# A chunked scan and a feed-forward layer on one core: the lead-in issued from one written list

## The chip, the core and the metric

The kernel runs on one core of a Trainium2 chip. The core has a matrix engine, TensorE (PE in the rows, with its weight loads as PEld), a vector engine, VectorE (DVE), a scalar engine, ScalarE (ACT), GpSimd (POOL), and SyncE (SP), which only issues transfers here. Each engine works through its own list of instructions in order; semaphores make one wait for another. The metric is the device time in microseconds (us), median of several runs of the same program.

## The reference

Two layers stand one behind the other. The first is a scan over 768 positions with a decay for each, for 4 batches and 8 heads of 32 columns (D), with a state of 16 x 32 for each head (N = 16). The reference does it in chunks:

```
log_a = log(clip(a, 1e-6, 1));  cum = cumsum(log_a) inside a chunk
L = exp(cum_i - cum_j) for i >= j, else 0
y = ((C B^T) * L) x  +  exp(cum_i) * (C state)
state = exp(cum_end) * state + sum_j exp(cum_end - cum_j) B_j x_j
```

The second takes the 3072 tokens of 256 columns that the first gives, and computes `g = max(0.01 h, h)` with `h = x @ w_in` (256 to 2048 columns), and then `g @ w_out` (2048 to 256).

## The kernel before

**The scan** goes in 16 chunks of 48 positions, 0 to 15, one behind the other, since each needs the state of the one before. A chunk takes these steps, with the lines of before:

- decays: ones are added up by matmuls to sums of logarithms (`sc` or `pd` in PSUM), and ScalarE takes the exponential to `lt`. Chunks 0 to 2 are "direct": VectorE fills tiles `reach` (L595) that a matmul turns into sums (L272 to L299). Chunks 3 and on take their sums from rows in DRAM: the sums are computed once (`sums`), split into three bf16 parts (`split_sums`), stored (`left_d`, `right_d`, L240 and L244), and loaded for each chunk as small rows `dl` and `dr` (L253 and L256) into one of SLOTS = 2 places. A "decay block" is the pair of matmuls of L280 that works on them. ScalarE fills the rest of such a place with constants (L209, "a fill").
- scores: C B^T of all heads, 32 matmuls (L336, "score block"); C comes in with the chunk's input `bcn`. Each head's C has to stand in its own half of the partitions with zeros in the other. Chunks 0 to 2 get a narrow C, which ScalarE copies twice with a factor of 0 or 1 for each partition (`spread_c`, L315, into `cs`); the other chunks get it spread from the host, as a wider input `d_l`.
- weigh: VectorE multiplies scores by decays, into `lt` (L350); GpSimd does the same for the part of the state (L321).
- chunk products: 64 matmuls `lt` by `xs` (L366).
- handing on: VectorE transposes the new state into `stage` (L396), and eight small copies put it into the next chunk's `xs` (L412); before, ScalarE, VectorE and GpSimd share them by a written tuple.
- the result goes to `xh` (L423, rounded to the high part) and `xl` (L431, the rest), the tokens of the second layer.

**The feed-forward layer** works on tiles of 512 tokens (t, 6 of them) and blocks of 128 of the 2048 inner columns (f, 16 of them), in *steps* 0, 1, 2 and on of one (t, f) each. The first steps are tile 0 with the weight blocks 0 to 5; they need chunks 0 to 2 only. For each step there are: the first-layer product, six matmuls of 512 columns into `hp` (L522); the leaky activation into `gh` (L529) and `hp` (L532) on ScalarE; the low part `gl` on VectorE (L535); and the second-layer product, six matmuls into `op` (L546), some steps later. The weights come as 64-bit words, and are decoded once per block: magnitude (L450 on ScalarE or L463 on VectorE), shift, sign and low word on VectorE (L468 to L477), then the high part `wh` on ScalarE (L490) and the low part `wl` on GpSimd (L491).

**Order.** The program is written out in the order in which each engine runs it; nothing is moved by a scheduler. Before, a straight piece of code (L575 to L713, "the lead-in") issues the work up to the third chunk, and then a loop over the steps issues each step with what goes beside it: the chunks' products, the decays two chunks ahead, the decoding. In its first five steps (EARLY) the loop takes other branches than later. Two more matmuls on a tile of zeros stand ahead of step 1's product (BRIDGE, issued by `keep_warm`, L119, "the bridging matmuls").

**Transfers** all go through SyncE's one queue: inputs `bcn` (three buffers), `xs` (two buffers), weights `raw` (three buffers), the rows. A transfer into a buffer that is still in use makes SyncE wait, with all that is behind it.

## Time and profile before

| | |
|---|---|
| median of 3 runs | 304.93 us (304.08 to 305.57) |
| the profiled execution | 303.38 us, of which the span from the first to the last instruction is 301.5 us |
| TensorE busy | 293.6 us, 97% of the span, 2718 instructions |
| VectorE busy | 218.3 us, 72%, 379 instructions |
| ScalarE busy | 182.4 us, 61%, 351 instructions |
| GpSimd busy | 71.9 us, 24%, 148 instructions |
| transfers | 22.95 MB, mean 76 GB/s |

The shares are means over the whole span. In the page's 40 slices (7.5 us each) TensorE has 8 or 9 tenths in all but the last, GpSimd stops after the 15th, and the transfers move 160 to 315 GB/s in the first eleven slices and little later: the chunks and the decoding of weights lie in the first part, and only the feed-forward layer in the rest. So the stage around the change, the first seventh, has to be read for itself.

### The profile page before, as it was taken

How to read it: one execution, taken by the hardware profiler on the slowest of the kernel's cores; microseconds unless marked ns; L12 is line 12 of the kernel's file. 1: busy time of each engine (PE TensorE's matmuls, PEld its weight loads, DVE VectorE, ACT ScalarE, POOL GpSimd, SP SyncE). 2: the span in 40 equal slices, each digit the busy share in tenths (PEclk: the TensorE clock that was granted, in tenths of full speed). 3: DMA queues.
4: the chain of work that ended last, by engine and by line, in shares of the span. 5: the costliest groups of instructions: out<-in, count | busy, mean ns of one | idle time of the engine just before them, and what ended most of it. 6: DMA issues, size and time to landing. Idle time of an engine off the chain costs nothing.

```text
span 301.5 us, 6819 instructions
## 1 busy us (share of the span) xinstructions
PE 293.6 (97%) x2718; PEld 230.9 (77%) x2718; DVE 218.3 (72%) x379; ACT 182.4 (61%) x351; POOL 71.9 (24%) x148
## 2 busy tenths in 40 slices
PE   8889999999999999999999999999999999999995
PEld 4547676777777778888888888888888888888883
DVE  6879979987875688866877887677576565656562
ACT  6989758666755565735555666574665364536452
POOL 7567666866865440000000000000000000000000
PEclk9999999999999999999999999999999999999999
DMA  6697658665532101000100000000030000000004
GB/s 235 213 315 245 199 173 252 206 222 174 161 93 93 28 5 67 0 2 0 70 2 1 0 0 3 0 0 0 2 139 0 0 2 1 0 0 2 0 0 139
DMA packets 12492, 22.95 MB, mean 76 GB/s; under 512 B 4590, under 2 KB 5486, under 8 KB 12462
## 3 DMA queue, kind: packets, MB, share of 16 engines
q1 hardware_dynamic: 12462, 22.53, 23.2%
q8 instruction: 21, 0.34, 0.5%
q14 instruction: 9, 0.07, 0.1%
HBM read 19.08 MB, written 3.44 MB: 75 GB/s over the span
## 4 chain that ended last, share of the span: by engine, by line
PE 89%; DVE 5%; ACT 2%; issue 1%; DMA 1%; POOL 0%; SPq 0%; DVEq 0%
PE sc L776 18%; PE op L806 14%; PE sc L806 14%; PE op L546 14%; PE hp L522 13%; PE hp L776 7%; PE sc L366 3%; PE sc L336 2%; PE sc L280 1%; DVE mag L463 1%; DVE top L468 1%; DMA dr<-right_d 1%; DVE w L477 1%; DVE gl L535 1%; DVE lt L350 1%
## 5 line engine op out<-in xcount | busy, mean ns | idle before, releaser
L412 POOL COPY xs<-stage 16x128 f32<-16x128 f32 x98 | 35.8, 365 | 24.5 <-DVE stage L396 18.2
L529 ACT ACTIVATE gh<-hp 128x512 fp32r<-128x512 f32 x32 | 19.1, 598 | 26.0 <-PE hp L522 25.8
L817 ACT ACTIVATE gh<-u 128x512 fp32r<-128x512 f32 x32 | 20.0, 625 | 17.7 <-DVE u L858 17.7
L546 PE MATMUL op<-gh,wh 128*128 128x512 f32 x64 | 27.9, 436 | 0.0
L821 DVE TENSOR_TENSOR gl<-u,gh 128x512 fp32r<-128x512 f32 x32 | 22.0, 687 | 7.9 <-ACT u L818 7.9
L857 DVE TENSOR_TENSOR u<-sc,kept 128x512 f32<-128x512 f32 x16 | 11.1, 691 | 22.2 <-PE sc L776 22.2
L817 ACT ACTIVATE gh<-kept 128x512 fp32r<-128x512 f32 x16 | 10.1, 633 | 28.1 <-DVE kept L866 28.1
L817 ACT ACTIVATE gh<-hp 128x512 fp32r<-128x512 f32 x16 | 9.6, 598 | 26.8 <-PE hp L776 26.8
L546 PE MATMUL op<-gl,wh 128*128 128x512 f32 x64 | 25.2, 394 | 0.4 <-DVE gl L535 0.4
L866 DVE TENSOR_TENSOR kept<-sc,kept 128x512 f32<-128x512 f32 x16 | 11.1, 692 | 19.4 <-PE sc L776 19.3
L546 PE MATMUL op<-gh,wl 128*128 128x512 f32 x64 | 25.0, 390 | 0.0
L806 PE MATMUL op<-gl,wh 128*128 128x512 f32 x64 | 24.9, 389 | 0.0
L806 PE MATMUL sc<-gl,wh 128*128 128x512 f32 x64 | 24.9, 389 | 0.0
L806 PE MATMUL sc<-gh,wl 128*128 128x512 f32 x64 | 24.9, 389 | 0.0
L806 PE MATMUL op<-gh,wh 128*128 128x512 f32 x64 | 24.9, 389 | 0.0
L806 PE MATMUL op<-gh,wl 128*128 128x512 f32 x64 | 24.9, 389 | 0.0
L806 PE MATMUL sc<-gh,wh 128*128 128x512 f32 x64 | 24.9, 389 | 0.0
L350 DVE TENSOR_TENSOR lt<-sc,lt 128x384 f32<-128x384 f32 x32 | 16.3, 550 | 10.7 <-ACT gh L529 8.1
L535 DVE TENSOR_TENSOR gl<-hp,gh 128x512 fp32r<-128x512 f32 x32 | 21.7, 677 | 3.1 <-ACT hp L532 3.1
L491 POOL TENSOR_TENSOR wl<-w,wh 128x512 fp32r<-128x512 f32 x16 | 20.7, 1301 | 9.6 <-ACT wh L490 9.4
L522 PE MATMUL hp<-xh,wh 128*128 128x512 f32 x64 | 20.3, 398 | 0.8 <-ACT xh L423 0.6
L818 ACT ACTIVATE u<-u 128x512 f32<-128x512 f32 x32 | 20.2, 632 | 1.0
(147 smaller groups left out, 733.1 us busy)
## 6 DMA issues: line engine op xcount, KB each, us to landing
raw<-w_l SPq DMA_DIRECT2D x16, 512.0 KB, 4.1
bcn<-d_l SPq DMA_DIRECT2D x13, 448.0 KB, 5.1
xs<-x_l SPq DMA_DIRECT2D x28, 96.0 KB, 3.4
out_l<-ob SPq DMA_DIRECT2D x10, 256.0 KB, 2.0
bcn<-c_l SPq DMA_DIRECT2D x3, 352.0 KB
xs<-x_l SPq DMA_DIRECT2D x2, 256.0 KB, 5.1
out_l<-ob SPq DMA_DIRECT2D x4, 128.0 KB
dl<-left_d SPq DMA_DIRECT2D x13, 9.0 KB, 3.7
```

Of the source, the lines that this page charges most:

```text
L350: nc.vector.tensor_tensor(out=to, in0=at, in1=to, op=ALU.mult)
L412: copy(xss[c + 1][h * R:h * R + N, 2 * p:2 * p + 2, bs], stage[rows, :, bs],)
L491: nc.gpsimd.tensor_tensor(out=wl[:, f], in0=w32s[f], in1=wh[:, f], op=ALU.subtract)
L522: nc.tensor.matmul(hp, lhsT=w_half[h][:, f, k * 128:(k + 1) * 128], rhs=x[t][:, k, :], start=(n == 0), stop=(n == 5),)
L529: nc.scalar.activation(ghs[s], hp, AF.Prelu, alpha=0.01)
L535: nc.vector.tensor_tensor(out=gls[s], in0=hps.pop(s), in1=ghs[s], op=ALU.subtract)
L546: nc.tensor.matmul(op, lhsT=w_half[h][:, f, DM + m * 128:DM + (m + 1) * 128], rhs=x, start=(start and i == 0), stop=(last and i == 2),)
L776: nc.tensor.matmul(bank, lhsT=w[h], rhs=x[g], start=start and i == 0, stop=i == 2, skip_group_check=True,)
L806: nc.tensor.matmul(outs[t][m], lhsT=w_half[h][:, f, DM + m * 128:DM + (m + 1) * 128], rhs=x, start=start and i == 0, stop=last and i == 2,)
L817: nc.scalar.activation(gh, h, AF.Prelu, alpha=0.01)
L818: nc.scalar.activation(in_place, h, AF.Prelu, alpha=0.01)
L821: nc.vector.tensor_tensor(out=gl, in0=g, in1=gh, op=ALU.subtract)
```

## The change

The lead-in and the first six steps are issued from one list of names, LEAD_IN; the loop begins at step 6. A name is a piece of work and a number (`p1` is the product of chunk 1, `hp0` the first-layer product of step 0, `w2` the transfer of weight block 2), and a letter behind a colon chooses the engine (A ScalarE, V VectorE, P GpSimd). With it:

- the masks of the decays of chunks 0 to 2 come first, also the sums of the far chunks (`rev`);
- the decays of chunks 4 and 5 stand in one double block behind the first-layer product of step 0 (`hp0 ... dec4 ... dec5`), where before those of chunk 4 stood behind the product of step 1, and those of chunk 5 behind that of step 2;
- C comes spread for all chunks; `spread_c` with its copies, and the tile `mine` and its making, are gone; the inputs of chunks 0 to 2 are as wide as the others;
- `xs` has three buffers, and the x of chunk 1 comes without the rows that a state will overwrite;
- the two bridging matmuls are gone;
- engines change for some work: the fill `reach4` to GpSimd, a clearing `top0`, the rest fills of chunks 3 and 4 (`fr4:A`, `fr3:P`), the hand-on copies of chunks 0 to 5, and `wl` of the blocks 1 and 5 to VectorE.

```diff
-OUT_AT = {1: 0, 2: 1, 3: 2, 4: 3, 5: 4, 8: 5}
+OUT_AT = {8: 5}
-BRIDGE = {1: 2}
+BEGIN, DONE = 6, 7
...
+AT_ONCE = ["la", "c0", "c1", "x0", "w0"]
+LEAD_IN = """
+clampf after clampn mask0 lnf mask1 lnn sums less reach1:V reach0:V fl0 rev sel cols
+reach3:V revn erevn cast0 direct0 exp0 rest reach2:V erevf sd0 top1:P sc0 cast1 x1
+weigh0 c2 reach4:P direct1 mask2 part2 exp1 top0:P save0 p0 abs0 reach5:V turn0 h6:A sc1
+h7:A shift0 w1 weigh1 h1:P x2 fl1 h4:P h2:V h0:A highs0 sign0 h5:A direct2 lows0 sd1
+low0 w2 exp2 h3:P fr4:A p1 abs1 rows3 sc2 sd2 turn1 h11:A fr3:P shift1 h9:P weigh2 h10:A
+h15:A c3 w3 h13:A sign1 low1 h12:P h14:A h8:P highs1 p2 dec3 rows4 turn2 sc3 wh0 abs2
+lows1 highs2 wh1 lows2 h22:V wl0:P rows5 x3 shift2 c4 hp0 h17:P exp3 h18:A h16:A weigh3
+c5 dec4 w4 sign2 dec5 h19:P h21:P wl1:V sd3 abs3 h20:P h23:A shift3 gh0 low2 sign3 rows6
+exp4 act0 exp5 hp1 p3 wh2 low3 wl2:P gh1 w5 wh3 save1 gl0 x4 sc4 turn3 op0 act1 highs3
...
+"""
...
-    pxs = scan.enter_context(tc.tile_pool(name="pxs", bufs=2))
+    pxs = scan.enter_context(tc.tile_pool(name="pxs", bufs=3))
-    pcs = early.enter_context(tc.tile_pool(name="pcs", bufs=2))
...
     def fetch_c(c, eng=nc.sync):
-        ins[c] = pin.tile([128, FAR], F32, name="bcn")
-        if c < SPREAD:
-            eng.dma_start(ins[c][:, :NEAR], c_l[c])
-        else:
-            eng.dma_start(ins[c], d_l[c - SPREAD])
+        ins[c] = pin.tile([128, ALL], F32, name="bcn")
+        eng.dma_start(ins[c], c_l[c])
...
-        for rows in [slice(h * R + N, h * R + R) for h in range(2)] if c > 1 else [slice(0, 2 * R)]:
+        for rows in [slice(h * R + N, h * R + R) for h in range(2)] if c else [slice(0, 2 * R)]:
...
-    def spread_c(c):
-        if c >= SPREAD:
-            spread[c] = ins[c][:, C_AT:].rearrange("p (b e i) -> p b e i", b=NB, e=2)
-            return
-        cs = spread[c] = pcs.tile([128, NB, 2, Q], F32, name="cs")
-        src = ins[c][:, C_AT:NEAR].rearrange("p (b i) -> p b i", b=NB)
-        for e in range(2):
-            nc.scalar.activation(cs[:, :, e], src, AF.Copy, scale=mine[:, e:e + 1])
...
     def scores(c, space):
-        cs = spread[c]
+        cs = ins[c][:, C_AT:].rearrange("p (b e i) -> p b e i", b=NB, e=2)
...
+    for name in LEAD_IN.split():
+        if name in acts:
+            acts[name]()
+            continue
+        name, _, eng = name.partition(":")
+        kind = name.rstrip("0123456789")
+        i = int(name[len(kind):])
+        if eng:
+            chosen[kind](i, engines[eng])
+        else:
+            numbered[kind](i)
...
-    for s in range(total):
+    for s in range(BEGIN, total):
         c = out_at.get(s)
-        n = PASSES[s] if s < len(PASSES) else 4
-        ffn_in(s, BRIDGE.get(s, 0))
+        n = PASSES if s < NF + 3 else 4
+        ffn_in(s)
+        ffn_high(s)
```

What the list changes in the order of the instructions shows best in three places. In the rows a number behind a name tells buffers apart.

TensorE, from the product of chunk 2 (`pd<-lt,xs`) to the first-layer product of step 1, before; the three `hp` rows of a product read xh by wh, xl by wh, xh by wl:

```order
L366 MATMUL pd_421<-lt_337,xs_280 32x64 x32
L522 MATMUL hp_489<-xh_328,wh_163 128x512 x2
L522 MATMUL hp_489<-xl_329,wh_163 128x512 x2
L522 MATMUL hp_489<-xh_328,wl_164 128x512 x2
L280 MATMUL sc_501<-dr_133,dl_132 128x384
L336 MATMUL sc_504<-bcn_289 64x96 x16
L119 LDWEIGHTS idle_101
L119 MATMUL hp_548<-idle_101 128x512
L522 MATMUL hp_548<-xh_328,wh_163 128x512 x2
```

The same place after (line numbers of the changed kernel):

```order
L377 MATMUL pd_404<-lt_322,xs_300 32x64 x32
L301 MATMUL sc_437<-dr_124,dl_123 128x384
L346 MATMUL sc_444<-bcn_392 64x96 x16
L536 MATMUL hp_489<-xh_307,wh_144 128x512 x2
L536 MATMUL hp_489<-xl_308,wh_144 128x512 x2
L301 MATMUL sc_508<-dr_124,dl_123 128x384
L301 MATMUL sc_514<-dr_124,dl_123 128x384
L536 MATMUL hp_539<-xh_307,wh_144 128x512 x2
```

The decays (`sc<-dr,dl`) and the scores (`sc<-bcn`) of chunk 3 have moved ahead of step 0's product, the decays of chunks 4 and 5 (two tiles, 508 and 514) stand between step 0 and step 1, and the bridging matmuls on `idle` are gone.

SyncE's queue, from the storing of the sums on, before:

```order
L240 DMA left_d_161<-parts_159 128x2x144
L244 DMA right_d_162<-parts_159 128x288
L112 DMA xs_280<-x_l 48x512 x2
L94 DMA raw_283<-w_l 128x2048
L253 DMA dl_132<-left_d_161 48x2x48
L256 DMA dr_133<-right_d_162 6x16x48
L103 DMA bcn_289<-d_l 128x896
L94 DMA raw_396<-w_l 128x2048
```

And after:

```order
L261 DMA left_d_142<-parts_140 128x2x144
L265 DMA right_d_143<-parts_140 128x288
L112 DMA raw_295<-w_l 128x2048
L131 DMA xs_300<-x_l 48x512 x2
L112 DMA raw_320<-w_l 128x2048
L274 DMA dl_123<-left_d_142 48x2x48
L277 DMA dr_124<-right_d_143 6x16x48
L122 DMA bcn_392<-c_l 128x896
L112 DMA raw_394<-w_l 128x2048
```

Two weight blocks (`raw_295`, `raw_320`) instead of one now stand ahead of the rows and of the fourth chunk's input (`bcn`, of c_l after), and only the rows of chunk 3 ahead of that input, where before those of chunk 4 stood there too.

ScalarE, from the first hand-on copy of chunk 0 to the copies of the high parts of chunk 2, before:

```order
L412 COPY xs_117<-stage_316 16x2x64 x3
L423 CAST xh_328<-pd_247 128x2x192
L450 ACTIVATE mag_331<-raw_119 128x512
L315 ACTIVATE cs_334<-bcn_121,mine_131 128x4x48 x2
L299 ACTIVATE lt_337<-pd_308 128x2x4x48 x2
L209 COPY dr_133<-later_126 48x384
L412 COPY xs_280<-stage_403 16x2x64 x3
L423 CAST xh_328<-sc_344 128x2x192
L623 ACTIVATE erev_158<-pd_308 128x80
L490 CAST wh_163<-w32_418 128x512
L423 CAST xh_328<-pd_421 128x2x128
```

The same after:

```order
L421 COPY xs_215<-stage_273 16x2x64 x2
L203 COPY dr_124<-less_121 96x384
L430 CAST xh_307<-sc_237 128x2x192
L320 ACTIVATE lt_322<-pd_227 128x2x4x48 x2
L227 COPY dr_124<-later_119 48x384
L457 ACTIVATE mag_360<-raw_295 128x512
L421 COPY xs_300<-stage_382 16x2x64 x5
L430 CAST xh_307<-pd_327 128x2x192
L495 CAST wh_144<-w32_318 128x512
L457 ACTIVATE mag_462<-raw_320 128x512
L430 CAST xh_307<-pd_404 128x2x128
```

The first magnitude has moved ahead of the hand-on copies (it is not in the second piece), a fill (L203) has come in between them, five copies instead of three are done for chunk 1, the spreading copies (`cs`) are gone, and the magnitude of the second weight block (`raw_295`) stands ahead of chunk 1's hand-on copies.

## Rows read from the trace of the kernel before

**Rows 1.** Page, part 2: granted TensorE clock in 40 slices, in tenths.

```profile
PEclk9999999999999999999999999999999999999999
```

**Rows 2.** Windows: window, us, busy PE, PEld, DVE, ACT, POOL, clock, DMA share, GB/s.

```profile
42.35:300.00 257.65, 255.09 (x1985) 205.70 (x1983) 182.33 (x301) 148.04 (x267) 44.71 (x94) 1.00 0.15 49
```

**Rows 3.** Timeline of TensorE: start, busy us, engine, line, operation [idle before <-releaser].

```profile
8.43 0.86 PE L366 MATMUL pd<-lt,xs 64*32 64x64 f32 x64 [0.30 <-POOL lt L321]
...
11.28 1.16 PE L366 MATMUL sc<-lt,xs 64*32 64x64 f32 x64
...
14.99 0.83 PE L366 MATMUL pd<-lt,xs 64*32 64x64 f32 x62 [0.24 <-ACT xh L423]
16.42 0.73 PE L522 MATMUL hp<-xh,wh 128*128 128x512 f32 x2 [0.60 <-ACT xh L423]
...
19.41 0.60 PE L119 MATMUL hp<-idle 128*128 128x512 bf16 x2
...
42.35 0.62 PE L522 MATMUL hp<-xh,wh 128*128 128x512 f32 x2
```

**Rows 4.** Chain that ended last, 40 to 61 us: start, us, engine and line.

```profile
40.11 0.82 PE sc L336 x32
...
49.68 1.38 PE op L546 x6
51.06 1.36 PE hp L522 x6
52.42 0.79 PE sc L366 x53
53.21 1.60 PE op L546 x6
...
60.48 0.43 PE sc L280 x2
```

**Rows 5.** Timeline of ScalarE, 9 to 14 us.

```profile
9.81 0.94 ACT L412 COPY xs<-stage 16x128 f32<-16x128 f32 x3 [0.30 <-DVE stage L396]
10.65 0.46 ACT L423 CAST xh<-pd 128x384 fp32r<-128x384 f32 x1
11.14 0.68 ACT L450 ACTIVATE mag<-raw 128x512 bf16<-128x512 bf16 x1
11.73 0.79 ACT L315 ACTIVATE cs<-bcn,mine 128x192 f32<-128x192 f32 x2
12.42 0.84 ACT L299 ACTIVATE lt<-pd 128x384 f32<-128x384 f32 x2
13.16 0.50 ACT L209 COPY dr<-later 48x384 f32<-48x384 f32 x1
```

**Rows 6.** Timeline of VectorE and GpSimd, at 8 and at 33 us.

```profile
8.25 0.55 DVE L595 TENSOR_TENSOR reach<-la,upto 112x384 f32<-112x384 f32 x1
...
32.88 1.30 DVE L463 TENSOR_SCALAR mag<-mag 128x512 uint16<-128x512 uint16 x1
...
7.75 1.52 POOL L321 TENSOR_TENSOR lt<-bcn,erev 128x256 f32<-128x256 f32 x2 [0.89 <-ACT erev L610]
...
32.73 1.30 POOL L491 TENSOR_TENSOR wl<-w,wh 128x512 fp32r<-128x512 f32 x1 [2.13 <-ACT wh L490]
```

**Rows 7.** Timeline of SyncE's queue, 6 to 11 us.

```profile
6.77 0.39 SPq L240 DMA_DIRECT2D left_d<-parts  x1
...
9.32 1.47 SPq L112 DMA_DIRECT2D xs<-x_l  x2
```

**Rows 8.** Windows, columns as in Rows 2.

```profile
2.00:9.00 7.00, 6.70 (x126) 3.48 (x127) 5.90 (x18) 5.21 (x16) 5.72 (x15) 1.00 0.94 325
...
18.50:22.00 3.50, 3.09 (x41) 1.78 (x40) 2.20 (x6) 3.37 (x8) 2.94 (x5) 1.00 1.02 270
```

**Rows 9.** Page, part 6: issues, KB each, median us from issue to landing.

```profile
bcn<-d_l SPq DMA_DIRECT2D x13, 448.0 KB, 5.1
...
dl<-left_d SPq DMA_DIRECT2D x13, 9.0 KB, 3.7
```

More of the change, by code (lines that the diff above doesn't have):

```diff
@@ L485, in scan_ffn, with weights_high, weights_low @@
     pending = []
+    def weights_high(f):
+        nc.scalar.copy(wh[:, f], w32s[f])
+    def weights_low(f, eng):
+        eng.tensor_tensor(out=wl[:, f], in0=w32s[f], in1=wh[:, f], op=ALU.subtract)
+        ready.add(f)
     def settle():
@@ L489, in settle @@
             f = pending.pop(0)
-            nc.scalar.copy(wh[:, f], w32s[f])
-            nc.gpsimd.tensor_tensor(out=wl[:, f], in0=w32s[f], in1=wh[:, f], op=ALU.subtract)
-            ready.add(f)
+            weights_high(f)
+            weights_low(f, nc.gpsimd)
     def do_low(f):
@@ L499, in do_low @@
             fetch_w(f)
[L501 removed]
+    for f in range(DONE, NF):
         passes.extend(((g, f) for g in (decode_shift, decode_sign, do_low)))
@@ new lines, in scan_ffn, with deep_banks, clamp, log @@
+    deep = ExitStack()
+    ps_d = deep.enter_context(
+        tc.tile_pool(name="ps_d", bufs=2, space=PSUM, reuse_waits="tile")
+    )
+    def deep_banks():
+        return ps_d.tile([128, 2, TS], F32, name="pd")
+    near_far = dict(n=slice(0, near), f=slice(near, NC * NM))
+    def clamp(part):
+        cols = near_far[part]
+        nc.vector.tensor_scalar(
+            out=la[:, cols], in0=la[:, cols], scalar1=1e-6, scalar2=1.0, op0=ALU.max,
+            op1=ALU.min,
+        )
+    def log(part):
+        cols = near_far[part]
+        nc.scalar.activation(la[:, cols], la[:, cols], AF.Ln)
@@ L616, in reverse, with reverse_near, reverse_far @@
+    NEAR_AT, FAR_AT = 2 * Q, 2 * Q + near // 2
+    def reverse_near(space):
+        for k in range(2):
+            for g in range(2):
+                h, rows = half(g, 2 * k), slice(g * R, g * R + Q)
+                nc.tensor.matmul(
+                    space[h * R:(h + 1) * R, k, NEAR_AT:FAR_AT], lhsT=after[rows, g],
+                    rhs=by_pair(la[:, :near], rows, k), start=True, stop=True,
+                )
+    def reverse_far(space):
+        for h, cols in enumerate(rest_of):
             nc.tensor.matmul(
-                space[:, at:at + cols.stop - cols.start],
+                space[:, h, FAR_AT:FAR_AT + cols.stop - cols.start],
@@ L620, in reverse, with reverse_exp @@
             )
-        def reverse_exp(space, cols, at):
+    rest_of = [slice(max(h * 128, near), (h + 1) * 128) for h in range(2)]
+    def reverse_exp(part, space):
+        if part == "n":
             nc.scalar.activation(
-                erev[:, cols], space[:, at:at + cols.stop - cols.start], AF.Exp
-            )
-        fill_columns()
-        for top in tops:
-            nc.gpsimd.memset(top.rearrange("p c h -> p (c h)").bitcast(F32), 0.0)
-        pds = [free_tile() for _ in range(2)]
@@ L631, in scan_ffn @@
-        for pd in pds:
-            decay_mask(pd)
-        fill_reach(0, 0)
-        fill_reach(0, 1)
-        sums(first)
-        decay_direct(0, pds[0])
-        nc.vector.tensor_reduce(out=mine, in_=own, axis=mybir.AxisListType.X, op=ALU.add)
-        fill_reach(2, 0)
-        splitting = split_sums(first)
-        next(splitting)
-        spread_c(0)
-        fill_reach(1, 0)
-        next(splitting)
-        for _ in splitting:
-            pass
-        fill_reach(1, 1)
-        save_sums(0)
@@ new lines, in scan_ffn, with place, do_mask, do_stack @@
+    pds, scs, oss = {}, {}, {}
+    ps_o = ps_h = None
+    engines = dict(A=nc.scalar, V=nc.vector, P=nc.gpsimd)
+    def place(pool):
+        return deep_banks() if pool == "d" else banks()
+    def do_mask(c):
+        pds[c] = place(PD[c])
+        decay_mask(pds[c])
+    def do_stack(c):
+        pds[c] = banks()
+        decay_stack(c, pds[c])
+    def do_scores(c):
+        scs[c] = banks()
+        scores(c, scs[c])
+    def do_products(c):
+        oss[c] = place(OS[c]) if c < DIRECT else banks()
+        chunk_products(c, oss[c])
@@ new lines, in do_in, with zero_top @@
+    def do_in(s):
+        nonlocal ps_o, ps_h
+        if ps_h is None:
+            deep.close()
+            ps_o, ps_h = (
+                ctx.enter_context(tc.tile_pool(name=n, bufs=2, space=PSUM, reuse_waits="tile"))
+                for n in ("ps_o", "ps_h")
+            )
+        ffn_in(s)
+    def zero_top(i, eng):
+        eng.memset(tops[i].rearrange("p c h -> p (c h)").bitcast(F32), 0.0)
+    acts = dict(
+        after=select_after, less=select_less, sel=select_sel, cols=fill_columns,
+        revn=lambda: reverse_near(first), sums=lambda: sums(first),
+        rev=lambda: reverse_far(first), erevn=lambda: reverse_exp("n", first),
+        erevf=lambda: reverse_exp("f", first), cast0=lambda: sum_part(0, first),
+        rest=lambda: sum_rest(first), cast1=lambda: sum_part(1, first),
+        part2=lambda: sum_part(2, first),
+    )
```

356 lines of the change are left out of this document (120 added, 236 removed).

## The prediction

> **What bounds the kernel now.** I began with the granted clock, which stands at full in all forty slices [rows 1], so no time is lost there. Next I asked where TensorE stops being the bound. From 42.35 us to the end it is busy 255.09 of 257.65 us, while VectorE has 182.33 and ScalarE 148.04 [rows 2]. The matmul at 42.35 is the first one of the first-layer product of step 6 [rows 3]. From this product on, both programs list the same TensorE instructions. So a change in the lead-in is worth what it moves this product, and I work out its start alone.
>
> The TensorE rows ahead of it show two stretches [rows 3]. The first goes to 16.42, where the first-layer product of step 0 starts; it holds the first three chunks, whose products start at 8.43, 11.28 and 14.99, and here ScalarE, VectorE and GpSimd hand the state from chunk to chunk. The second, 16.42 to 42.35, is 25.93 us long. What it has to do, by the pieces of the chain [rows 4]: six first-layer products of 1.36, three chunk products of 0.79, four score blocks of 0.82, four decay blocks of 0.43, five second-layer products (1.38 and 1.60 occur, I take the mean 1.49), and the two bridging matmuls, 0.60 [rows 3]. That is 8.16 + 2.37 + 3.28 + 1.72 + 7.45 + 0.60 = 23.58, so 2.35 us of the stretch are waits and slips. All that a better order can win is these 2.35, the 0.60, and what the first stretch loses.
>
> **The change, part by part.**
>
> *Removed.* Six spreading copies on ScalarE, 0.69 for a pair (11.73 to 12.42 [rows 5]), so 2.1 us of an engine that is packed here. The selection on GpSimd and the reduction that fed them lie beside other work. The two bridging matmuls, 0.60.
>
> *Added to the queue.* Each of the first three inputs grows by 96 KB, and the second x input shrinks by 64 KB: 224 KB more before anything else. In the stretch 2 to 9 us the queue moved 325 GB/s at 94% busy [rows 8], so this is 0.7 us of transfer. Work stands in front of it for the first chunk; for what is queued behind, see below.
>
> *The first stretch.* I place ScalarE's rows of after one behind the other. The masks and the far decays come ahead of the first chunk product: 0.43 for a mask (a decay block has the same shape), about as much for the far decays, less the 0.30 wait that stood there. I take 8.7 for its start. In before, 1.38 us pass from there to the first hand-on copy (8.43 to 9.81, [rows 3, 5]); so 10.1. ScalarE then does four hand-on copies (0.28 each), a fill (0.50) and the copy of the high parts (0.49) before the next product can start: 2.11, so 12.2, 0.9 later than now. Then one exponential pair (0.74), a fill (0.50), the first step of the second weight block (0.59) and five hand-on copies (1.40): 15.4 for the third product, 0.4 later. Behind it ScalarE has a copy of high parts, a weight copy (0.55, between the 0.49 of 384 columns and the 0.59 of 512), a magnitude and the last high parts, to about 17.7. Without the queue the first first-layer product would start there, 1.3 us later than now. In that time the order has put one decay block and one score block ahead of it (1.25), so this is no loss.
>
> *The queue.* That score block needs the input of the fourth chunk. Now, SyncE stores the sums at 6.77, and then holds everything back until the first chunk product has freed a place for the third x input, 9.32 [rows 7]. After, a third x buffer removes that wait, and the second and third weight block go ahead of the fourth chunk's input. But the sums are stored only behind the first weighing, at about 8.7. Ahead of and with this input stand, in MB of 10^6: 0.13 + 3 x 0.46 + 0.26 + 0.20 + 0.52 = 2.49, sums 0.15, two weight blocks 1.05, x 0.20, rows 0.02, itself 0.46: 4.36. At 325 GB/s from 2.0 on they end at 15.4, which is a lower bound, since small packets and landing come on top. The other way: it is issued behind the two loads of decay rows, which wait for the stored sums, at about 13; from issue to landing such an input takes 5.1 us in the median [rows 9]; so 18.1. I take 18.0, nearer to the second, since the 5.1 has other transfers in front of it as this one will. Score block 0.82: the first-layer product starts at 18.8.
>
> *The second stretch.* One score block and one decay block less and no bridge: 23.58 - 0.82 - 0.43 - 0.60 = 21.73. The new double decay block stands behind the first product. Its second half needs rows whose place only comes free when the fourth chunk's decays are done, at about 16.8; they are issued to 17.5 and take 3.7 [rows 9], so 21.2 at the worst, against 18.8 + 1.36 + 0.43 = 20.6 when TensorE gets there. I put in 0.4. Two second weight halves go from GpSimd (1.30, [rows 6]) to VectorE; no row shows them there. Bounds are 0.55 (a row of 384 columns of the same operation) and 1.30; I take 0.65. They lie beside the products, as does the fill on GpSimd (bounds 0.28, a hand-on copy, and 1.30). I leave 0.25 for slips, against 1.95 in before, since the order puts each activation a product ahead. Sum: 18.8 + 21.73 + 0.65 = 41.2.
>
> *The sum.* 42.35 - 41.2 = 1.15 us less; I say 1.2. The profiled execution took 303.38 us, its span 301.5 and 1.9 around it; after would be 302.2. The median of the runs, 304.93, lies 1.55 above it, and so I add the difference to that: **303.7 us**.
>
> **A rule against it.** One of six fills of the reach tiles goes to GpSimd. In before such a fill on VectorE took 0.55 at 8.25, while GpSimd ran tensor operations from 7.75 to 9.27 [rows 6]; what was held up beside GpSimd was the magnitude step, 1.30 at 32.88 while GpSimd's weight half ran [rows 6]. So I let the fill cost VectorE nothing. The Trainium skill, GPSIMD Engine Reference, section Specifications, says that GpSimd shares its memory interface with VectorE and that instructions with two SBUF inputs contend too. By that the fill, and the last sum behind it, would end up to 1.0 us later, and the stores and all behind them too: 304.7. The 0.55 row speaks against it, the 1.30 row for the other half of the rule.
>
> **Rivals.**
> *The queue keeps up.* If the fourth input lands by 16.9, the first product starts at 17.9 and the rows for the double block are there: 17.9 + 21.73 + 0.25 = 39.9, a gain of 2.45: 302.5. For it: 4.36 MB at full rate end at 15.4. Against: 5.1 us to landing.
> *The queue falls behind.* At the 270 GB/s that it moved from 18.5 to 22, as busy as it can be [rows 8], the part behind the first 2.49 MB ends 1.2 us later, the second weight block holds up ScalarE ahead of five hand-on copies, and the rows of the double block are late by as much: the gain is gone, 304.9.
> *The clock falls.* From 11.1 on (8.7 + 0.79 + 0.82 and the third chunk's decays) the order leaves TensorE idle 1.1 us before the second chunk product, 1.6 before the third and 1.4 before the score block, with small tiles between, and the two bridging matmuls are gone. The gaps noted now are 0.30, 0.24 and 0.60 [rows 3], and the clock stays at its upper level, 2.4 GHz [rows 1]. At 1.2 GHz each us of matmul takes two. From the third chunk product to the end of the second first-layer product stand 0.79 + 0.43 + 0.82 + 2 x 1.36 + 0.86 = 5.6 us, of which some 1.3 hide in the wait for the input: 4.3 more, so 303.7 + 4.3 = 308.0; it decides once the lower level holds for more than 1.2 us of work on the path. No row of before shows the lower level. The Trainium skill, TensorE: Matmul & The Clock Gate, Part 1, has the lower level as the default, which activity lifts; by that rule sparse stretches are a risk.
>
> **How the numbers follow.** A measurement of this kernel tells about 0.5% (1.5 us) from no change: 303.4 and 306.5 are the bounds. Forecast 0.53 (its own range 302.9 to 304.5, four tenths of it below 303.4); queue keeps up 0.20; queue falls behind, with the rule on the interface, 0.15; clock 0.12. Faster: 0.21 + 0.20 = 0.41. Slower: 0.12 and a tail of 0.02, 0.14. Same: the rest, 0.45. The range leaves out the best part of the second case and most of the clock: 302.2 to 306.0.
>
> **What would show it.** The first-layer product of step 0 near 18.8, behind the score block that waited for its input; step 6 near 41.2 with under 1 us of waits between; the second chunk product near 12.2 and the third near 15.4, each behind a hand-on copy of ScalarE; a short wait for rows in the double block; the clock at full. I am wrong if the score block waits for nothing, if the stretch from step 0 to step 6 is longer than 23 us, or if TensorE waits anew behind step 6.

## The result, and the profile after

The changed kernel takes 306.26 us in the median of 22 runs (303.8 to 311.59), the kernel before 303.88 (22 runs, 302.85 to 306.27). The ratio is 1.0064, with an interval of 1.0043 to 1.0085; it leaves out disturbed runs, which the medians hold. So it is slower by a little more than the 0.5% that a measurement tells from no change (the interval begins at 0.43%). Forecast were 303.7 and a range of 302.2 to 306.0. The forecast was counted down from 304.93, the median of three runs; over 22 runs the kernel before is 1.05 us faster than that.

The page of the changed kernel (TensorE's granted clock in 40 slices of 7.6 us, in tenths) stands against [rows 1]:

```profile
PEclk9957999999999999999999999999999999999999
```

In the third and fourth slice TensorE was granted half its clock, 1.2 instead of 2.4 GHz, in part of the time. Every one of the 22 runs shows it: the mean clock over the span is 0.983 to 0.992, where the profile of before has 1.0. The kernel before is not wholly free of it: of its 79 runs that stand beside the experiments below, 75 have a mean clock of 0.998 or more, and four have 0.987 to 0.994. The windows say when (window, us, busy PE, PEld, DVE, ACT, POOL, granted clock, DMA share, GB/s):

```profile
14.00:16.00 2.00, 0.07 (x4) 0.00 (x0) 0.25 (x2) 0.72 (x2) 1.04 (x4) 0.99 0.72 252
16.00:18.00 2.00, 1.04 (x41) 0.87 (x43) 1.97 (x5) 1.89 (x7) 0.00 (x0) 0.50 1.00 312
20.00:24.00 4.00, 4.00 (x38) 2.93 (x32) 3.64 (x10) 2.54 (x7) 1.78 (x6) 0.50 0.61 179
24.00:28.00 4.00, 4.00 (x75) 2.73 (x74) 2.58 (x4) 3.53 (x8) 0.02 (x1) 0.72 0.90 288
28.00:32.00 4.00, 3.98 (x53) 3.05 (x44) 3.07 (x7) 2.77 (x7) 3.77 (x6) 1.00 0.95 287
```

From 14 to 16 us TensorE did next to nothing (0.07 of 2 us), and from 16 to about 26 us it had the lower level. Its timeline (start, busy us, engine, line, operation, and in brackets the wait ahead and who ended it), to be held against [rows 3]:

```profile
8.92 0.86 PE L377 MATMUL sc<-lt,xs 64*32 64x64 f32 x64
11.90 1.35 PE L377 MATMUL pd<-lt,xs 64*32 64x64 f32 x64 [0.50 <-POOL lt L331]
13.18 0.89 PE L346 MATMUL sc<-bcn 32*64 32x96 f32 x32
16.96 1.69 PE L377 MATMUL pd<-lt,xs 64*32 64x64 f32 x64 [2.89 <-DVE lt L360]
18.74 0.82 PE L301 MATMUL sc<-dr,dl 102*128 102x384 bf16 x2
19.68 1.72 PE L346 MATMUL sc<-bcn 32*64 32x96 f32 x32
21.33 1.22 PE L536 MATMUL hp<-xh,wh 128*128 128x512 f32 x2
...
45.89 0.63 PE L536 MATMUL hp<-xh,wh 128*128 128x512 f32 x2
```

The chunk products start at 8.92, 11.90 and 16.96. The third has waited 2.89 us, within which the level fell (at 15.97 by the trace's record of the clock), and from there on the same blocks take up to twice as long: a score block 1.72 instead of 0.89. The first-layer product of step 0 starts at 21.33, that of step 6 at 45.89, 3.5 us later than before, and the span is 3.3 us longer. Behind step 6 nothing differs: 304.8 - 45.89 = 258.9 us, before 301.5 - 42.35 = 259.1.

What was late ahead of the third product is read from three engines: the magnitude of the second weight block on ScalarE, the shift and the weighing on VectorE, and the queue:

```profile
15.25 0.65 ACT L457 ACTIVATE mag<-raw 128x512 bf16<-128x512 bf16 x1 [1.58 <-DMA raw<-w_l]
15.93 1.53 ACT L421 COPY xs<-stage 16x128 f32<-16x128 f32 x5
...
15.94 0.29 DVE L470 TENSOR_SCALAR mag<-mag 128x512 uint16<-128x512 uint16 x1 [1.75 <-ACT mag L457]
16.15 1.02 DVE L360 TENSOR_TENSOR lt<-sc,lt 128x384 f32<-128x384 f32 x2
...
9.14 0.40 SPq L261 DMA_DIRECT2D left_d<-parts  x1
10.10 1.60 SPq L112 DMA_DIRECT2D raw<-w_l  x1
11.74 0.89 SPq L131 DMA_DIRECT2D xs<-x_l  x2
12.68 0.42 SPq L112 DMA_DIRECT2D raw<-w_l  x1
13.20 0.38 SPq L274 DMA_DIRECT2D dl<-left_d  x1
14.10 0.36 SPq L122 DMA_DIRECT2D bcn<-c_l  x1
```

The storing of the sums (9.14) holds back all that is queued behind it. The second weight block is issued at 10.10 and is there at 15.25. ScalarE's five hand-on copies stand behind its magnitude, and VectorE's weighing for the third product behind its shift. That is how a late weight block, which no chunk needs, starves TensorE. The third x is not far ahead of it: by its semaphores it has landed at 15.56 and 16.05 us, one time for each half.

### The profile page after: what moved, and what is told of

It is laid out like the page before. It is cut to its first block, busy times and chain, and to the rows that moved or that the text cites. A ratio compares the mean times of both kernels' runs of the same rounds, so it can differ in the third digit from the quotient of the medians.

```text
span 304.8 us, 6806 instructions
## 1 busy us (share of the span) xinstructions
PE 296.2 (97%) x2716; PEld 234.1 (77%) x2716; DVE 213.9 (70%) x378; ACT 181.7 (60%) x349; POOL 66.2 (22%) x141
## 3 DMA queue, kind: packets, MB, share of 16 engines
q1 hardware_dynamic: 12446, 22.76, 23.4%
## 4 chain that ended last, share of the span: by engine, by line
PE 95%; DMA 2%; SPq 1%; DVE 0%; ACT 0%; issue 0%
PE sc L790 18%; PE op L563 15%; PE hp L536 15%; PE op L820 14%; PE sc L820 14%; PE hp L790 7%; PE sc L377 3%; PE sc L346 3%; PE sc L301 2%; DMA dl<-left_d 2%; SPq L112 1%; PE sc L138 1%; PE pd L283 0%; ACT lt L320 0%; PE sc L242 0%
## 5 line engine op out<-in xcount | busy, mean ns | idle before, releaser
L421 POOL COPY xs<-stage 16x128 f32<-16x128 f32 x93 | 31.8, 342 | 28.9 <-DVE stage L408 25.0
L831 ACT ACTIVATE gh<-kept 128x512 fp32r<-128x512 f32 x16 | 10.1, 632 | 28.1 <-DVE kept L880 28.1
L536 PE MATMUL hp<-xh,wh 128*128 128x512 f32 x64 | 21.3, 415 | 0.0
L498 POOL TENSOR_TENSOR wl<-w,wh 128x512 fp32r<-128x512 f32 x14 | 18.4, 1326 | 13.0 <-ACT wh L495 12.8
```

Of the source, the lines that this page charges most:

```text
L421: copy_on(eng)(xss[c + 1][h * R:h * R + N, 2 * p:2 * p + 2, bs], stages[c][rows, :, bs])
L498: eng.tensor_tensor(out=wl[:, f], in0=w32s[f], in1=wh[:, f], op=ALU.subtract)
L536: nc.tensor.matmul(hp, lhsT=w_half[h][:, f, k * 128:(k + 1) * 128], rhs=x[t][:, k, cols], start=(n == 0), stop=(n == 5),)
L831: nc.scalar.activation(gh, h, AF.Prelu, alpha=0.01)
```

## The experiments

All ratios are to the kernel before, on the same chip; they are not the quotients of the medians, which the two groups of run times (last section) move by up to 0.4%. Where a time in us after the start is given, it is from one profiled execution; executions of the same kernel differ there by up to 2 us (last section).

**1. Is the lower clock the loss?** Twelve matmuls on the tile of zeros fill the idle time ahead of the third product.

```diff
+FILL = {'p2': 12}
...
         oss[c] = place(OS[c]) if c < DIRECT else banks()
+        keep_warm(oss[c][:, 1], FILL.get(f"p{c}", 0))
```

> Twelve matmuls on the tile of zeros ahead of the third chunk product, where the changed kernel lets TensorE stand idle for 2.89 us. Theory clock (TensorE starved, then ran at the lower level from 16 us to about 26 us, and that is most of the loss): granted clock at full in all slices, third product still near 17.0, first-layer product of step 0 near 20.4 instead of 21.3, step 6 near 42.6 instead of 45.9; time about that of before, ratio 0.998 to 1.003. Theory queue (the late transfers alone cost the time): TensorE still waits for the same transfers and the ratio to before stays at 1.006 or above.

Measured: 304.81 us, ratio 1.0038 (1.0009 to 1.0067). The clock is at 0.999 or 1.0 in 11 of 12 runs. TensorE's timeline:

```profile
13.88 2.76 PE L139 MATMUL pd<-idle 128*128 128x512 bf16 x12
16.57 1.20 PE L378 MATMUL pd<-lt,xs 64*32 64x64 f32 x64
18.54 0.48 PE L302 MATMUL sc<-dr,dl 102*128 102x384 bf16 x2 [0.78 <-DMA dr<-right_d]
19.71 0.89 PE L347 MATMUL sc<-bcn 32*64 32x96 f32 x32 [0.69 <-DMA bcn<-c_l]
20.53 0.73 PE L537 MATMUL hp<-xh,wh 128*128 128x512 f32 x2
...
42.97 0.40 PE L537 MATMUL hp<-xh,wh 128*128 128x512 f32 x1
```

The third product starts 0.4 us earlier (16.57 against 16.96), about as much as the first one does (8.43 against 8.92), and yet step 6 starts at 42.97 instead of 45.89. From the third product to step 6 it takes 26.4 us instead of 28.9, so in these two profiles the clock cost 2.5 us. Over the runs it is less: the two ratios differ by 0.26%, 0.8 us, their intervals overlap, and the interval here reaches into the ranges of both theories, so the run times alone do not decide between them. The profile of the changed kernel has one of the lowest mean clocks, 0.983; 0.989 is the commonest. What is left is the queue: the decay rows and the fourth input make TensorE wait 0.78 and 0.69 us.

**2. Is it the two bridging matmuls?** They are put back into the changed kernel, and taken out of the kernel before.

```diff
+BRIDGE = {1: 2}
...
+        keep_warm(hp, BRIDGE.get(s, 0))
```

> The changed kernel with the two bridging matmuls back ahead of the first-layer product of step 1, alone. Theory clock: the clock has fallen long before that place, so nothing is gained; lower level again from about 16 us, ratio 1.005 to 1.010. Theory bridge (the clock falls for want of these two): clock at full, ratio 0.999 or less.

Measured: 306.64 us, ratio 1.0092 (1.0066 to 1.0119), clock 0.982 to 0.989 in all six runs. In the kernel before:

```diff
-BRIDGE = {1: 2}
+BRIDGE = {}
```

> The kernel before without its two bridging matmuls, alone. Theory that starving as long as 2.9 us is what brings the lower level: the longest wait of TensorE here is 0.6 us, or 1.2 without the bridge, so the clock stays at full and the time falls by 0 to 0.6 us, ratio 0.998 to 1.000. Theory bridge: lower level in some runs, clock 0.98 to 0.99, ratio 1.005 or more.

Measured: 303.34 us, ratio 0.9998 (0.9973 to 1.0024), clock 0.999 or 1.0 in all 12 runs. The bridge has no part in the clock. Nor does it cost anything that shows before. TensorE's first-layer products of steps 0 and 1, without it and then in the profile of before (its step 0 is in [rows 3]):

```profile
17.80 0.73 PE L522 MATMUL hp<-xh,wh 128*128 128x512 f32 x2 [0.60 <-ACT xh L423]
...
21.55 0.73 PE L522 MATMUL hp<-xh,wh 128*128 128x512 f32 x2 [0.70 <-ACT wh L490]
...
20.17 0.73 PE L522 MATMUL hp<-xh,wh 128*128 128x512 f32 x2 [0.16 <-ACT wh L490]
```

They are 3.75 us apart without it as with it (16.42 to 20.17). The 0.60 us lay in a wait for weights.

**3. Does starving bring the lower clock in the kernel before too?** One transfer is moved there.

```diff
-        fetch_x(2)
         fetch_w(1)
         load_rows(3)
         load_rows(4)
         fetch_c(3)
+        fetch_x(2)
```

> The kernel before with one transfer moved: the third x input goes behind the second weight block, the rows and the fourth input, so that the third chunk product has to wait for it some 2.5 us longer; nothing else is changed, the bridging matmuls stay. Theory clock: TensorE starved that long brings the lower level in most runs of this kernel too, and the loss is the wait and 2 to 3.4 us more, ratio 1.010 to 1.020. Theory that the lower level comes from something else in the change: clock at full, loss of the wait alone, ratio 1.005 to 1.009.

Measured: 307.33 us, ratio 1.0083 (1.0054 to 1.0112). By size alone this is the other theory's (1.005 to 1.009); but that theory has the clock at full, and it fell in most runs. The ten runs fall apart by themselves: in seven the mean clock is 0.986 to 0.989, and they take 307.19 to 307.88 us; in three it is 0.999 or 1.0, and they take 305.02 to 305.57. Against the 303.66 us of the kernel before, the runs without the lower level cost about 1.8 us more (median 305.49), and those with it another 2.0 (307.50). A row of TensorE, and two windows, from one of the seven:

```profile
18.27 1.29 PE L366 MATMUL pd<-lt,xs 64*32 64x64 f32 x64 [3.54 <-DMA xs<-x_l]
...
16.00:18.00 2.00, 0.00 (x0) 0.00 (x0) 0.39 (x1) 0.57 (x1) 1.26 (x1) 0.50 0.85 290
18.00:20.00 2.00, 1.29 (x64) 1.07 (x64) 0.00 (x0) 0.40 (x2) 0.00 (x0) 0.50 1.03 327
```

The level fell at 15.78 us, while TensorE waited. That is the cleanest sign that starving is the cause: one transfer moved, the lower level in seven of ten runs where the kernel before on the same chip has no run under 0.992, and the loss doubles where the clock falls. No profile of one of the three other runs was kept, so that TensorE waited as long in them is not shown.

**4. Is it the wait for the weight block on the two engines?** The decoding of that block moves behind the weighing and the hand-on copies (`abs1 shift1 sign1 low1` behind `highs1`); the queue stays.

```diff
-... p1 abs1 rows3 ... fr3:P shift1 h9:P weigh2 ... h13:A sign1 low1 h12:P ... highs1 p2
+... p1 rows3 ... fr3:P h9:P weigh2 ... h13:A h12:P ... highs1 abs1 shift1 sign1 low1 p2
```

> The changed kernel with the decoding of the second weight block moved behind the weighing and the hand-on copies of the third chunk on ScalarE and VectorE, so that nothing of the chain waits for that block; the queue as it is. Third product near 15.5 instead of 17.0, but the rows of the fourth chunk still land near 18.7, so the starving only moves behind the third product (2 us and more). Theory clock: lower level as before, ratio 1.003 to 1.008, no gain beyond 0.5 us. Theory that the wait for the weight block is the cause: clock at full and ratio 0.998 or less.

Measured: 307.0 us, ratio 1.0123 (1.0087 to 1.0158), clock 0.983 to 0.989 in all five runs. TensorE now waits three times:

```profile
16.10 1.28 PE L377 MATMUL pd<-lt,xs 64*32 64x64 f32 x64 [1.59 <-DMA dr<-right_d]
17.31 0.50 PE L301 MATMUL sc<-dr,dl 102*128 102x384 bf16 x2
18.64 1.75 PE L346 MATMUL sc<-bcn 32*64 32x96 f32 x32 [0.83 <-DMA bcn<-c_l]
21.40 1.19 PE L536 MATMUL hp<-xh,wh 128*128 128x512 f32 x2 [1.01 <-ACT xh L430]
```

The third product starts 0.9 us earlier than in the changed kernel, at 16.10. The view names the rows for its wait, but this product does not read them; a step of the next transfer on the same semaphore falls at that time. The third x, the one transfer that it waits for, had landed at 14.59 and 14.88 us by its semaphores. What came last are the hand-on copies, and they stand behind VectorE's transposition:

```profile
14.52 0.43 DVE L408 STREAM_TRANSPOSE stage<-pd 128x256 f32<-128x256 f32 x1
14.98 1.53 ACT L421 COPY xs<-stage 16x128 f32<-16x128 f32 x5 [0.85 <-DVE stage L408]
15.08 0.97 POOL L421 COPY xs<-stage 16x128 f32<-16x128 f32 x3 [2.14 <-DVE stage L408]
```

VectorE has worked without a pause from 10.84 us on, where it had waited 1.03 us for the magnitude of the first weight block. So with the second block out of the way the engines' own order holds the third product, with a late transfer further back, and behind it the fourth input (0.83 us) and a copy of high parts (1.01 us) hold step 0, which starts no earlier than in the changed kernel (21.40 against 21.33). The wait for the weight block was not the whole cause, and moving its decoding alone gains nothing: the interval lies above that of the changed kernel. Two waits of 1.31 us (ahead of the second product) and 1.59 us were enough for the lower level here; it came at 17.79.

**5. Does the fourth input stand too far back?** As in experiment 1, with the third weight block behind the fourth input.

```diff
-low0 w2 exp2 ... c3 w3 ... wh0 abs2 ... wh1
+low0 exp2 ... c3 w2 w3 ... wh0 ... wh1 abs2
```

> The changed kernel with twelve matmuls ahead of the third chunk product, as in the first experiment, and one transfer moved: the third weight block goes behind the rows of chunk 3 and the fourth chunk's input (its magnitude behind the high parts of block 1). Theory queue: the fourth input lands near 18.0 instead of 19.7, its score block waits for nothing, first-layer product of step 0 near 19.0 instead of 20.5, step 6 near 41.5, ratio 0.997 to 1.000. If the input's late landing is hidden by other waits: step 0 stays at 20 or later, ratio 1.003 as without the move.

Measured: 304.44 us, ratio 1.0016 (0.9989 to 1.0042), clock at 0.997 or more in all 12 runs. TensorE's first chunk product, fourth score block and step 0:

```profile
10.67 0.86 PE L378 MATMUL sc<-lt,xs 64*32 64x64 f32 x64
...
20.85 0.89 PE L347 MATMUL sc<-bcn 32*64 32x96 f32 x32
21.67 0.73 PE L537 MATMUL hp<-xh,wh 128*128 128x512 f32 x2
```

The score block waits for nothing. The profiled execution started about 2 us late, as the last section tells, and so the times after its start don't compare; but the input is there 5.0 us behind its issue (15.57 to 20.56 by its semaphore) against 6.2 in experiment 1 (13.40 to 19.58), and from the first chunk product to the first-layer product of step 0 it takes 11.0 us (10.67 to 21.67) against 12.1 (8.43 to 20.53). From step 0 to step 6 it takes 0.9 more (23.4 against 22.4), so part of it is given back. The ratio lies between what the two theories gave, and its interval holds both ends. This is the best of the changed versions; it is level with the kernel before, not faster.

**6. Can the queue be put in order?** Three steps: the second weight block and the third x ahead of the stored sums, and the fourth input right behind them; the same with the decay rows earlier; and that with matmuls to fill.

```diff
-weigh0 c2 reach4:P ... save0 p0 ... w1 weigh1 h1:P x2 ... low0 w2 ... c3 w3 ... wh0 abs2
+weigh0 c2 w1 x2 reach4:P ... save0 c3 p0 ... weigh1 h1:P ... rows3 w2 ... w3 ... wh1 abs2
```

> The changed kernel with another order of the queue alone: second weight block and third x ahead of the storing of the sums, the fourth chunk's input right behind it, the rows and the third weight block after these; the magnitude of the third block behind the high parts of block 1. Theory queue: second weight block landed by 13.5 instead of 15.2, third chunk product near 15.5 instead of 17.0, score block of the fourth chunk waits for nothing, first-layer product of step 0 near 18.5; if the clock stays at full with it, step 6 near 40.7 and ratio about 0.995. Theory clock: the starving is shorter but not gone (some 1.5 us ahead of the third product); if the lower level still comes, step 6 near 44 and ratio 1.001 to 1.005.

Measured: 305.28 us, ratio 1.0052 (1.0029 to 1.0076).

```diff
-... rows3 w2 ... w3 ... rows4 ... rows5 x3
+... rows3 rows4 w2 ... rows5 w3 x3
```

> The changed kernel with the queue of the earlier experiment on it (second weight block and third x ahead of the storing of the sums, the fourth input behind it), and with the decay rows of chunk 4 right behind those of chunk 3, ahead of the third weight block, and those of chunk 5 ahead of the fourth. Theory queue: the double decay block waits less than 0.4 us instead of 1.3, and from the first-layer product of step 0 to that of step 6 it takes 22.5 us instead of 24.9; ratio near 0.998. Theory clock: no matmuls are added, so executions in which the lower level comes remain; clock 0.983 to 0.992 in some runs and ratio 1.000 to 1.004.

Measured: 307.03 us, ratio 1.0117 (1.0069 to 1.0165).

```diff
+FILL = {'p2': 4, 'dec4': 2}
```

> The same queue, with four matmuls on the tile of zeros ahead of the third chunk product and two ahead of the double decay block. If clock and queue together are the whole loss: clock at full in nearly all runs, first-layer product of step 0 near 18.5, step 6 near 41.0, ratio 0.994 to 0.998. If something else in the change costs time: ratio stays at 1.002 or more although the clock is at full.

Measured: 307.71 us, ratio 1.012 (1.0079 to 1.0161). The first comes out at the upper end of theory clock, with the mean clock under 0.995 in ten of twelve runs. The other two miss both theories (clock 0.982 to 0.998, and 0.992 to 0.994 in spite of the filling). The third shows why; TensorE's second product and the product of chunk 3:

```profile
11.79 1.14 PE L378 MATMUL pd<-lt,xs 64*32 64x64 f32 x42 [0.36 <-POOL lt L332]
14.96 0.42 PE L378 MATMUL pd<-lt,xs 64*32 64x64 f32 x22 [2.04 <-issue]
...
26.99 0.94 PE L378 MATMUL sc<-lt,xs 64*32 64x64 f32 x64 [2.12 <-ACT lt L326]
```

The second product breaks off behind 42 of its 64 matmuls and stands for 2.04 us, and no semaphore holds it ("issue"). The filling stands behind this place; the lower level comes at 16.02. The other wait is for the exponential of chunk 4's decays, which frees the PSUM place that this product takes. It stands on ScalarE behind the magnitude of the fourth weight block, and that block is late:

```profile
24.69 0.65 ACT L458 ACTIVATE mag<-raw 128x512 bf16<-128x512 bf16 x1 [1.88 <-DMA raw<-w_l]
...
26.06 0.83 ACT L326 ACTIVATE lt<-sc 128x384 f32<-128x384 f32 x2
```

**7. The inputs of the chain alone ahead.** Third x, stored sums, fourth input, and then the weight blocks and rows; without and with filling (six matmuls ahead of the third product, two ahead of the score block).

```diff
-... c2 reach4:P ... save0 p0 ... w1 weigh1 h1:P x2 ... p1 abs1 rows3 ... c3 w3 ... rows4
+... c2 x2 reach4:P ... save0 c3 w1 p0 ... weigh1 h1:P ... p1 rows3 rows4 w2 ... rows5 w3
```

> The changed kernel with the chain's inputs first: third x ahead of the storing of the sums, the fourth input right behind it, only then the second weight block, the rows of chunks 3 and 4, the third block; the decoding of the second block behind the high parts of chunk 2. The queue stays short while TensorE's own instructions are fetched at 10 us, unlike in the two earlier queue experiments, where TensorE stood 0.8 to 2.0 us in the middle of the second product without waiting for a semaphore. Theory queue: third product near 15.5, score block of the fourth chunk waits for nothing, first-layer product of step 0 near 18, step 6 near 40.5, ratio 0.993 to 0.998. Theory clock: where the starving is down to about 1 us, the level stays at full in most runs; if it falls in most runs all the same, ratio 0.999 to 1.003.

> The same with six matmuls on the tile of zeros ahead of the third chunk product and two ahead of the fourth chunk's score block. Theory clock: full in all runs, and faster than without them only where the lower level came there; theory that filling costs what it saves: equal or slower by up to 0.5 us than without them.

Measured: 308.15 us, ratio 1.0133 (1.0091 to 1.0174), and 306.35, ratio 1.0076 (1.0047 to 1.0105). The first misses both theories; the second is faster, with the clock at 0.987 to 0.999. With filling, step 0 starts at 18.69, near the forecast, but the double decay block then waits 2.4 us for the exponential of chunk 3, behind the decoding of two late weight blocks on ScalarE:

```profile
22.72 0.57 PE L302 MATMUL sc<-dr,dl 102*128 102x384 bf16 x2 [2.38 <-ACT lt L326]
```

So a second order of ScalarE's work was tried, with that exponential right behind the high parts of chunk 2; with the second weight block ahead of the fourth input; and without filling.

```diff
-... highs1 p2 ... wh0 lows1 highs2 lows2 abs1 shift1 sign1 low1 wh1 abs2 ... hp0 h17:P exp3
+... abs1 shift1 highs1 p2 ... wh0 lows1 highs2 lows2 low1 exp3 ... hp0 h17:P wh1 ... abs2
```

> The queue of the experiment before (third x ahead of the stored sums, fourth input and second weight block behind them) and its eight filling matmuls, with the exponential of chunk 3 no longer behind the decoding of the second and third block on ScalarE: it follows the high parts of chunk 2, the magnitude of the second block stands ahead of the high parts of chunk 1, that of the third behind the weighing of chunk 3. Theory queue and clock (these two are the whole loss, and the rest of the list works): first-layer product of step 0 near 18.8, double decay block waits 0.5 us at most instead of 2.4, step 6 near 41.2, ratio 0.994 to 0.999. Theory that the list keeps ScalarE and VectorE too full for its order: step 1 or 2 waits anew by 1 us or more, step 6 at 43 or later, ratio 1.002 or more.

> The same with the second weight block ahead of the fourth chunk's input. Step 0 later by up to 1.4 us, step 1 waits less for its weights; if the input is what holds step 0, ratio 0.001 to 0.004 above that of the run before it.

> The first of these three without the eight filling matmuls. Theory clock: lower level in part of the runs, clock 0.983 to 0.995 there, ratio 0.002 to 0.008 above the first; if filling is no longer needed, equal to it within 0.002.

Measured: 306.29 us, ratio 1.0088 (1.0052 to 1.0125); 305.8, 1.0086 (1.0052 to 1.012); 307.39, 1.0134 (1.009 to 1.0179). The first comes out in the ranges of its second theory (1.002 or more, step 6 at 43 or later; it starts at 45.64), that the list keeps ScalarE and VectorE too full. The second is not above the first, so the place of the fourth input against the second weight block tells nothing. The third is 0.0046 above the first, as theory clock had it. Without filling the clock is down in all six runs (0.983 to 0.994); with it, it is at 0.992 to 1.0. Four pairs of kernels differ by filling alone. In three the filled one is faster, by 0.26% (experiment 1 against the changed kernel), 0.57% and 0.46% (the two pairs here), none clear of the intervals alone; in the pair of experiment 6 it is not. The last profile:

```profile
18.48 0.70 PE L536 MATMUL hp<-xh,wh 128*128 128x512 f32 x2 [0.62 <-DVE xl L438]
...
23.66 0.94 PE L377 MATMUL sc<-lt,xs 64*32 64x64 f32 x64 [0.84 <-issue]
24.86 0.70 PE L346 MATMUL sc<-bcn 32*64 32x96 f32 x19 [0.26 <-ACT lt L325]
27.76 0.55 PE L346 MATMUL sc<-bcn 32*64 32x96 f32 x13 [2.19 <-issue]
```

Step 0 starts at 18.48, 0.3 earlier than forecast, and by 28 us the lead is gone. From 20 to 26 us the queue moves 343 to 353 GB/s at a full share, and from 25.6 us on TensorE stands again in the middle of a block with no semaphore to wait for. The lower level comes at 28.59, behind this stand and not ahead of the third product. In the two kernels with filling the product of chunk 3 waits 1.94 and 1.72 us for an exponential on ScalarE.

## Why the prediction was wrong

**What bounds the kernel: right.** From step 6 to the end it is 259.1 us before, 258.9 after, and 258.9 to 259.1 in the profiles of all the experiments; the start of step 6 is the whole difference.

**The first stretch: wrong at its third product.** Starts of 8.7, 12.2 and 15.4 were forecast; 8.92, 11.90 and 16.96 came. (The terms given for the first, 8.43 + 0.43 + 0.43 - 0.30, make 9.0 and not 8.7.) The step that failed is ScalarE's chain. It costed "the first step of the second weight block (0.59)" as work alone, as if the block were there; it is there 1.58 us after ScalarE is free. The release is not the one that was forecast either, a hand-on copy of ScalarE: the second product was let go by GpSimd's weighing, the third by VectorE's, which hangs on the same block by its shift. With the block out of this chain the third product starts at 16.10 (experiment 4), so this step explains about 0.9 of the 1.6 us; the third x, which lands at 15.56 and 16.05 in the changed kernel, and the hand-on behind VectorE explain why 15.4 was out of reach besides. The rival "queue falls behind" named just this place, and was given 0.15 together with the rule on the interface.

**The queue: mis-sized by 1.7 us.** The fourth input's score block was put at 18.0; with the clock at full it starts at 19.71 (experiment 1). The term was the issue at about 13, and 5.1 us to land. In that profile it is issued at 13.40 and has landed at 19.58, 6.2 us later; most of the error is in the landing. In the changed kernel the issue comes at 14.10, since the sums are stored at 9.14 and not at 8.7 and the first issue behind them takes 1.60 us, and it has landed at 19.54. Moving one weight block behind the input shortens the landing to 5.0 us and takes the wait away (experiment 5).

**The second stretch: right in its sum.** 21.73 + 0.65 = 22.4 us were forecast from step 0 to step 6, and 22.44 came with the clock at full (20.53 to 42.97). The 0.4 put in for rows did not come there, since step 0 was late enough for them. With the lower level it is 24.56. The price of 0.60 for the bridging matmuls was right in this sum, but the kernel before did not pay it (experiment 2): there it lay in a wait.

**The rule on the interface did not decide.** VectorE's fill at 6.97 us, beside a GpSimd that was busy from 6.59 to 8.93, took 0.66 us instead of 0.55 [rows 6], and its last sum began at 8.76. The Trainium skill, GPSIMD Engine Reference, section Specifications, has the two engines share an interface; of the 1.0 us that this was taken to be worth, 0.1 showed.

**The clock: the rival came true, its price was too high, and its total met by luck.** It was worked out as 4.3 us for the blocks from the third product to the second first-layer product. Measured are 2.5 us between the profiles of experiment 1 and the changed kernel. The lower level lasted to the place that was named, the second first-layer product, of which only the first two matmuls ran at it (1.27 us instead of 0.77); a score block took 1.72 instead of 0.89, a decay block only 0.82 instead of 0.48. The total of the profiled execution, 306.75 against 303.38 of before, is 3.4 us more; the rival had 308.0 against 304.93, 3.1 more. That these are near is luck: the 3.1 are 4.3 less a gain of 1.2 that did not come, the 3.4 are the clock and the late queue. What was wrong is its chance, 0.12. The gaps that the forecast itself put down (1.1, 1.6 and 1.4 us) were read as harmless since [rows 1] show the clock at full, but those rows come from a kernel whose longest gaps there were 0.30, 0.39, 0.24 and 0.60. The page of the Trainium skill that was named, TensorE: Matmul & The Clock Gate, Part 1, has the lower level as the default; the trace agrees, the level fell within a wait of 2.89 us.

**The two rivals were one.** The late queue starved TensorE, and the starving brought the lower clock. They were given as alternatives, each with the other absent. Their sum, by the prediction's own prices, is 304.9 + 4.3 = 309.2 at most, and the measured median lies between the first alone and both.

What stays open: why the ratio of experiment 1 is 1.0038, when its profile has step 6 only 0.6 us later than before (0.2%). Eleven of its twelve runs come in two groups as those of before do, six at 302.48 to 304.28 us and five at 305.33 to 306.59; the profile is from the lower, and the upper is a larger part here (five of eleven, against six of 23). Waits of the kind "issue" in the block of chunk 4's scores (0.2 us in that profile, 0.7, 1.8 and 2.2 in those of experiments 4, 2 and 7) come and go between executions, and would do too; which of the two it is, is not shown. Open too is why the mean clock of a run tells so little of its time: the runs of the changed kernel, all at 0.983 to 0.992, take 303.80 to 311.59 us.

## What to carry to other kernels

Price a wait on TensorE twice: what it costs while it lasts, and what the lower clock costs behind it; in experiment 3 a wait (3.5 us in its one profile) was followed by the lower clock in seven of ten runs, and there the loss doubled; twelve matmuls on zeros in the gap of the changed kernel, which cost nothing that shows there, kept the clock up in eleven of twelve runs. How short a wait is harmless these runs do not tell: two of 1.31 and 1.59 us in experiment 4 were not. When something is put into an engine's list ahead of the chain (here the decoding of a weight block), ask when its transfer lands and not how long it runs. When a queue is the bound, putting one transfer forward puts another back: five other orders of it let step 0 start as early as 18.48 us instead of 21.33, and none of the kernels came out faster than the one before.

## What the runs showed of the hardware

**TensorE stops with no semaphore to wait for, and goes on behind the landing of instructions.** On the page of the changed kernel there are 21 transfers of the kind "instruction" on queue 8, 0.34 MB in all, 16 KB each. Its matmuls and weight loads are 2716 each. In the three kernels of experiment 6, which put more data into the queue before 12 us, the second product stood for 0.8, 0.8 and 2.0 us in its middle with no semaphore to wait for; in the changed kernel, whose queue moved 96 GB/s between 10 and 12 us, it did not. The traces have the times of these transfers. In the changed kernel one runs from 9.96 to 11.31 us. In the third of the three kernels it runs from 12.48 to 13.62, though TensorE is as far (first chunk products at 8.92 and 8.94); the queue moved 391 and 270 GB/s there in the two us from 10, and TensorE goes on at 14.96. All the profiles together have 13 such stops of more than 0.3 us, and ten of them end 1.2 to 1.6 us behind the landing of such a transfer; three (1.65, 0.84 and 0.31 us) do not. That the fetch is held up behind the data and TensorE waits for it is the likeliest reading; it was not tried by itself.

**The clock first rises at different times.** In some executions the first matmul blocks run at double length for longer. The trace's records of the granted clock begin with the upper level at 4.1 to 6.0 us in twelve of the sixteen profiles, and at 9.8 to 10.1 in four; ahead of the first record the page prints the clock as full, so it does not show this. The first score block in the profile of experiment 2's second kernel, TensorE:

```profile
6.44 1.55 PE L336 MATMUL sc<-cs,bcn 32*64 32x96 f32 x32
...
10.59 0.89 PE L336 MATMUL sc<-cs,bcn 32*64 32x96 f32 x32
```

A block of this shape takes 1.55 us at 6.44 and 0.89 at 10.59; the record of the clock begins between them, at 10.08, and in the profile of before at 5.99. Its step 0 starts at 17.80 against 16.42 in the profile of before. The runs of the kernel before come in two groups, near 303.3 and near 305 us; that this late rise is what parts them fits their distance, and was not shown run by run.
